# An attention stage woven into a mixture of experts on one core: value products moved to later steps, sums of the first block taken earlier, transposes cut into 64-row halves

## The chip, the cores and the metric

The kernel runs on one core of a Trainium2 chip. The metric is the device time of one execution in microseconds (us), lower is better. Several runs of one kernel are taken and their median is quoted.

## The reference, cut to what matters

Three layers follow each other: a gated linear attention, a mixture of four experts, and a gated two-layer network.

```
for t in range(S):                       # attention: B=4, H=8 heads, S=768, D=48
    state = alpha[:, :, t, :, None] * state + einsum('bhd,bhe->bhde', k[:, :, t], v[:, :, t])
    y[:, :, t] = einsum('bhd,bhde->bhe', q[:, :, t], state)
x = y.transpose(0, 2, 1, 3).reshape(3072, 384)
p = domain_probs / (domain_probs.sum(-1) + 1e-9)
out = sum over e of p[:, e] * (relu(x @ w1[e]) @ w2[e])    # 4 experts, 384 -> 1024 -> 384
h = out @ w_in                                             # 384 -> 2048
return (h * clip(h + 3, 0, 6) / 6) @ w_out                 # 2048 -> 384
```

All of it is float32. The kernel splits each float32 operand of the two networks into a high and a low part, and makes three TensorE products of the parts.

## The kernel before

**The two networks** work on 6 blocks of 512 tokens. A step takes 128 hidden columns: `mm1` (L800) makes nine products into the tile `ph`, ScalarE writes the high part `hh` (L808), VectorE the low part `hl` (L811), and `mm2` (L859), one step later, makes nine products of `hh` and `hl` into the sums `po`. In `mm2` the third product of each column group is the first that reads `hl`. Steps on one expert are a visit; at its end `finish` multiplies the sums by the routing weight on VectorE (L902: t<-po,pb), which also frees the `po` banks for the next visit. In phase 0 every block takes 14 steps, a visit of 8 and one of 6. Block 0 is run as two halves of 256 tokens, 14 short steps each, since its tokens come from attention only little by little. The `ph` of block 0 has two banks, later ones have one, so that there `mm1` waits for `hl` of the step before.

**The attention** is cut into 12 units of 256 positions (3 for each batch). The class `Attention` writes its work as named pieces, in three tables of seven entries each (L48 to L56). Entry k of `GROUP` and `BETWEEN` is issued at the end of a step, and entry k of `CHUNK` in the step behind it, after that step's `mm1` and its `hl`. So a unit takes seven steps, which are called k0 to k6 here. A sign says whose piece it is: `-` the unit before, `+` the unit after. What the pieces do:

- k0 and k1: `T_tp`, `T_k`, `T_q` transpose alphas, keys and queries on TensorE into PSUM (ptt, pkt, pqt); ScalarE copies them to SBUF in a scattered order (L313, L328). `L2 L3` and `ST` (L458, L479) finish the output `py` of the unit before. `X` is a pair of one-column ScalarE copies (`met`, L471) for which `ST` waits. `tls` is on VectorE.
- k1 to k4: `Sc` copies `kc`, `qc` on ScalarE (L346), `Su` scales `kt`, `qt` in place on VectorE (L356, two instructions), `C` makes the score products (L368), one level of a tree per step. `Su0` waits for the copies of `T_q`, since `kc` stands behind them on ScalarE.
- `M0`, `M2` mask the scores (L380), `K` transposes keys back (pk, L392), `U` makes state updates into `pu` (L404), which reuses the bank that M2 reads, `Z` chains four states on VectorE (L427, L433), `Y` transposes `y8` by pairs of 64-row products (py, L442).
- In `CHUNK`: `y0` to `y5` are the products with the values (L253 to L280), which need `Y` of k6 only; `p`, `r`, `u`, `kk`, `kq`, `tp` prepare the next unit (L190 to L247).

In all engines but GpSimd the instructions stand in the order of the program, so a piece delays whatever is issued behind it on its engine. Attention has four PSUM banks. Two hold `py` from k6 until the copy in `A` in the step of k2. At k0 the other two are the banks of `pu`, which `Z` reads last. Units 1 to 4 lie in block 0, units 5 to 11 in blocks 1 to 4; unit 0 is a prologue.

The loop over steps decides where the pieces go:

```
low = mm1(vi, f)
low()
if rest:
    at.rest(rest.pop(0))
...
if done:
    mm2(*done)
```

Of the kernel before, what the change touches and what calls it, by code (L numbers as in the profile page):

```python
# [18 lines left out]
P = 128  # L19


class Attention:
# [20 lines left out]
    U = 256  # L43
    W = (4, 8, 16, 32)
    T = 64
# [3 lines left out]
        "T_tp T_k0 -L2 -L3 T_k1", "-ST T_q0 T_q1", "C0", "C1", "C2", "C3 K0 K1", "U Y L0 L1",  # L49
# [5 lines left out]
        "y0 y1 y2 y3 y4 y5", "-A +p0 +r0", "+p1 +p2 +r1", "-R +u0", "+u1 +cp +kk +kq", "+tp +p3 +r2", "-XS",  # L55
# [235 lines left out]
    def tree(self, n):  # L291
# [7 lines left out]
        s = {"tls": [], "kc": {}, "qc": {}, "pas": {}, "asb": {}, "ktok": {}, "sb": []}  # L299
# [16 lines left out]
        def T(src, tag, half):  # L316
            if half == 0:
                s[tag] = wk(tag, [P, 2, NP, P])
            pt = self.ps(f"p{tag}{half}_{n}")
            for i in range(4):  # L320
                pe.transpose(pt[:, P * i : P * i + P], src[:, 4 * half + i].rearrange("p h d -> p (h d)"), self.ident)  # L321
            out = s[tag].rearrange("p j r (c i) -> p j i c r", i=8)[:, :, 4 * half : 4 * half + 4]
            src_ = pt.rearrange("p (i j c r) -> p j i c r", i=4, j=2, r=NP)
            for j in range(2):
                if n == 0 and tag == "qt":
                    nc.vector.tensor_copy(out[:, j], src_[:, j])
                else:
                    nc.scalar.copy(out[:, j], src_[:, j])  # L328
# [213 lines left out]
def tile_gla__then__moe__then__moe2(  # L542
# [497 lines left out]
    for vi, vv in enumerate(visits):  # L1040
# [16 lines left out]
        for f in range(len(vv["steps"])):  # L1057
# [85 lines left out]
```

## Time and profile before

| what | value |
|---|---|
| median of 3 runs | 1397.3 us (1396.82 to 1398.92) |
| profiled execution, own time | 1398.23 us |
| its span, first to last instruction | 1396.3 us |
| TensorE busy in the span | 1363.5 us (98%) |
| VectorE busy | 843.9 us (60%) |
| ScalarE busy | 453.2 us (32%) |
| mean granted TensorE clock | 0.99 of full speed |

The profile is of one execution. Busy shares are means over stages with quite different limits: attention ends at about 480 us of the span, block 0 at about 182 us. A wait in the rows stands in square brackets before an instruction, with what released it.

### The profile page before, as it was taken

Reading aid. Unit: us, or ns where it says so; the run is one execution under the profiler, and the core shown is the slowest. Engines: PE = TensorE matmul, PEld = TensorE weight load, DVE = VectorE, ACT = ScalarE, POOL = GpSimd, SP = SyncE. Lnnn points to the kernel's source line nnn. Section 1 sums busy time; section 2 is a strip of 40 time slices with the busy share of each in tenths; the row PEclk is TensorE's granted clock in tenths of the full one; section 3 lists DMA queues with packets and bytes.
Section 4 is the critical chain, followed back from the end, with each engine's and each line's share of the span. In section 5 each row is a group of like instructions: output and inputs, shape, how many; then the busy total and the mean of one; then the engine's idle time right before and its main releaser. Section 6 shows DMA issues by size and latency. Waiting matters only on the chain.

```text
span 1396.3 us, 25745 instructions
## 1 busy us (share of the span) xinstructions
PE 1363.5 (98%) x10674; PEld 1143.5 (82%) x10674; DVE 843.9 (60%) x1526; ACT 453.2 (32%) x821; POOL 83.3 (6%) x125
## 2 busy tenths in 40 slices
PE   7699999999999999999999999999999999999998
PEld 6688888888878888888888888888888888888898
DVE  8899977768776258757666666635543333334332
ACT  3555444443344133211111111113333333333333
POOL 2000000000000001121111111100000000000000
PEclk9889999999999999999999999999999999999999
DMA  6654554345442247524242332313302020202010
GB/s 195 175 146 134 156 140 121 99 119 144 134 120 80 75 148 233 162 64 140 64 130 86 96 109 84 117 64 121 102 0 46 1 46 0 46 1 46 1 23 23
DMA packets 156548, 132.31 MB, mean 95 GB/s; under 512 B 65040, under 2 KB 138256, under 8 KB 156432
## 3 DMA queue, kind: packets, MB, share of 16 engines
q1 hardware_dynamic: 156432, 130.68, 32.6%
q8 instruction: 83, 1.36, 0.4%
q14 instruction: 33, 0.27, 0.1%
HBM read 100.71 MB, written 34.65 MB: 97 GB/s over the span
## 4 chain that ended last, share of the span: by engine, by line
PE 89%; DVE 7%; issue 1%; DMA 1%; ACT 1%; SPq 0%; DVEq 0%
PE ph L800 41%; PE po L859 38%; PE po L861 2%; PE py L458 2%; PE py L479 1%; PE pa L368 1%; PE pu L404 1%; PE pkt L321 1%; DVE qt L356 1%; DVE kt L356 1%; PE pk L392 1%; DVE hl L811 1%; DVE asb L380 1%; PE pqt L321 1%; DVE dg L247 1%
## 5 line engine op out<-in xcount | busy, mean ns | idle before, releaser
L859 PE MATMUL po<-hl,w1h 128*128 128x512 f32 (+1 forms) x858 | 326.4, 380 | 6.5 <-DVE hl L811 6.5
L859 PE MATMUL po<-hh,w1h 128*128 128x512 f32 (+1 forms) x858 | 326.4, 380 | 4.6 <-DVE t L902 4.5
L859 PE MATMUL po<-hh,w1l 128*128 128x512 f32 (+1 forms) x858 | 326.0, 380 | 0.0
L808 ACT ACTIVATE hh<-ph 128x512 fp32r<-128x512 f32 (+1 forms) x206 | 117.5, 570 | 523.1 <-PE ph L800 515.9
L811 DVE SCALAR_TENSOR_TENSOR hl<-ph,hh 128x512 fp32r<-128x512 f32 (+1 forms) x206 | 134.5, 653 | 245.4 <-ACT hh L808 245.4
L800 PE MATMUL ph<-xh,w0h 128*128 128x512 f32 (+1 forms) x906 | 255.9, 391 | 2.7 <-ACT xh L775 2.4
L800 PE MATMUL ph<-xh,w0l 128*128 128x512 f32 (+1 forms) x906 | 247.6, 382 | 0.0
L800 PE MATMUL ph<-xl,w0h 128*128 128x512 f32 (+1 forms) x906 | 247.2, 381 | 0.2 <-DVE xl L776 0.2
L800 PEld LDWEIGHTS ph<-xh,w0l 128*128 128x128 f32 x906 | 167.8, 190 | 33.1
L800 PEld LDWEIGHTS ph<-xl,w0h 128*128 128x128 f32 x906 | 167.6, 190 | 33.2 <-DVE xl L776 0.5
L859 PEld LDWEIGHTS po<-hl,w1h 128*128 128x128 f32 x858 | 162.5, 189 | 38.0 <-DVE hl L811 7.4
L859 PEld LDWEIGHTS po<-hh,w1h 128*128 128x128 f32 x858 | 162.5, 189 | 35.6 <-ACT hh L808 2.9
L800 PEld LDWEIGHTS ph<-xh,w0h 128*128 128x128 f32 x906 | 163.4, 190 | 33.8 <-ACT xh L775 2.6
L859 PEld LDWEIGHTS po<-hh,w1l 128*128 128x128 f32 x858 | 162.6, 189 | 30.3
L823 DVE SCALAR_TENSOR_TENSOR g<-g,ph 128x512 f32<-128x512 f32 (+1 forms) x97 | 66.2, 684 | 170.9 <-ACT g L819 170.9
L819 ACT ACTIVATE g<-ph,three 128x512 f32<-128x512 f32 (+1 forms) x97 | 66.2, 684 | 184.8 <-PE ph L800 184.8
L826 DVE SCALAR_TENSOR_TENSOR hl<-g,hh 128x512 fp32r<-128x512 f32 (+1 forms) x97 | 66.5, 687 | 66.7 <-ACT hh L824 66.7
L824 ACT ACTIVATE hh<-g 128x512 fp32r<-128x512 f32 (+1 forms) x97 | 61.0, 630 | 74.6 <-DVE g L823 74.6
L669 POOL TENSOR_TENSOR sq<-hc 128x256 f32<-128x256 f32 x48 | 34.5, 718 | 634.7 <-DVE hc L668 632.7
L902 DVE TENSOR_TENSOR t<-po,pb 128x512 f32<-128x512 f32 (+1 forms) x82 | 52.6, 656 | 0.0
L346 ACT COPY kc<-kt 128x512 f32<-128x512 f32 x48 | 30.3, 631 | 63.2 <-PE pa L368 46.8
L684 POOL TENSOR_TENSOR a<-a,hc 128x256 f32<-128x256 f32 x48 | 38.8, 808 | 184.6 <-DVE hc L683 184.6
(106 smaller groups left out, 1210.5 us busy)
## 6 DMA issues: line engine op xcount, KB each, us to landing
rx<-x_d SPq DMA_DIRECT2D x36, 384.0 KB
vl<-vd SPq DMA_DIRECT2D x96, 96.0 KB
rw<-in_moe_w_dram SPq DMA_DIRECT2D x21, 384.0 KB
pb<-p_d SPq DMA_DIRECT2D x28, 256.0 KB
raw<-in_moe_w_in_dram SPq DMA_DIRECT2D x24, 256.0 KB
raw<-in_moe_w_out_dram SPq DMA_DIRECT2D x24, 256.0 KB
acc_d<-t SPq DMA_DIRECT2D x20, 256.0 KB
rq<-in_q_dram SPq DMA_DIRECT2D x24, 192.0 KB
```

What stands on the lines that cost most here:

```text
L346: nc.scalar.copy(c.rearrange("p x (b w) -> p (x b) w", w=self.W[l]), halves(z, l, x))
L669: nc.gpsimd.tensor_tensor(sq, hc, hc, op=mul)
L684: nc.gpsimd.tensor_tensor(a, a, hc, op=add)
L800: pe.matmul(ph[:, 0:n], w[:, j, fs], x[:, j, cs], start=(o == 0 and j == 0), stop=(o == 2 and j == KT - 1),)
L808: nc.scalar.activation(hh[:, 0:n], ph[:, 0:n], AF.Relu)
L811: nc.vector.scalar_tensor_tensor(hl[:, 0:n], ph[:, 0:n], 0.0, hh[:, 0:n].bitcast(F32), op0=ALU.max, op1=sub)
L819: nc.scalar.activation(g[:, c], ph[:, c], AF.Relu, bias=three)
L823: nc.vector.scalar_tensor_tensor(g[:, c], g[:, c], 6.0, ph[:, c], op0=ALU.min, op1=mul)
L824: nc.scalar.activation(hh[:, c], g[:, c], AF.Copy, scale=1.0 / 6.0)
L826: nc.vector.scalar_tensor_tensor(hl[:, c], g[:, c], 1.0 / 6.0, hh[:, c].bitcast(F32), op0=mul, op1=sub)
L859: pe.matmul(accs[vi][m][:, 0:n], w[:, z, ms], h[:, 0:n], **fl)
L902: nc.vector.tensor_tensor(t[:, 0:n], po[:, 0:n], pb, op=mul)
```

## The change

Three edits. In `CHUNK`, `y2` to `y5` leave entry 0 for entries 1 to 4, `kq` goes from entry 4 to 5, and the load of the next unit's values moves from entry 1 to entry 4, behind the last piece that reads them. In the loop, where a visit of block 0 ended with the step before, `mm2` with its sums is now issued ahead of the attention's `CHUNK` piece. `T` and `K` no longer make eight 128-row transposes in two halves, each with its own bank; they make 16 products of 64 rows, the upper 64 partitions into one bank and the lower into the other, in turn, and the copies follow after all 16. `T_k` now comes behind `L2 L3` as one piece.

```diff
@@ -46,13 +46,13 @@
     H = 7
 
     GROUP = (
-        "T_tp T_k0 -L2 -L3 T_k1", "-ST T_q0 T_q1", "C0", "C1", "C2", "C3 K0 K1", "U Y L0 L1",
+        "T_tp -L2 -L3 T_k", "-ST T_q", "C0", "C1", "C2", "C3 K", "U Y L0 L1",
     )
     BETWEEN = (
         "-X tls", "Sc0 Su0", "Sc1 Su1", "Sc2 M0 Su2", "Sc3 Su3", "M2", "Z0 Z1 Z2 Z3",
     )
     CHUNK = (
-        "y0 y1 y2 y3 y4 y5", "-A +p0 +r0", "+p1 +p2 +r1", "-R +u0", "+u1 +cp +kk +kq", "+tp +p3 +r2", "-XS",
+        "y0 y1", "-A +p0 +r0 y2", "+p1 +p2 +r1 y3", "-R +u0 y4", "+u1 +cp +kk y5", "+kq +tp +p3 +r2", "-XS",
     )
 
     def __init__(self, ctx, tc, q, k, v, alpha, y_d, psum_pool, psum_tag, reload, split):
...
@@ -313,19 +313,25 @@
                 nc.scalar.copy(out[:, j], src[:, j])
             s["tls"].append(tl)
 
-        def T(src, tag, half):
-            if half == 0:
-                s[tag] = wk(tag, [P, 2, NP, P])
-            pt = self.ps(f"p{tag}{half}_{n}")
-            for i in range(4):
-                pe.transpose(pt[:, P * i : P * i + P], src[:, 4 * half + i].rearrange("p h d -> p (h d)"), self.ident)
-            out = s[tag].rearrange("p j r (c i) -> p j i c r", i=8)[:, :, 4 * half : 4 * half + 4]
-            src_ = pt.rearrange("p (i j c r) -> p j i c r", i=4, j=2, r=NP)
+        def T(src, tag):
+            out = s[tag] = wk(tag, [P, 2, NP, P])
+            pts = [self.ps(f"p{tag}{j}_{n}") for j in range(2)]
+            for i in range(8):
+                for j in range(2):
+                    js = slice(64 * j, 64 * j + 64)
+                    pe.matmul(
+                        pts[j][:, 64 * i : 64 * i + 64],
+                        src[js, i].rearrange("p h d -> p (h d)"),
+                        self.ident[js, js],
+                        start=True, stop=True, is_transpose=True,
+                    )
             for j in range(2):
+                to = out[:, j].rearrange("p r (c i) -> p i c r", i=8)
+                from_ = pts[j].rearrange("p (i c r) -> p i c r", i=8, r=NP)
                 if n == 0 and tag == "qt":
-                    nc.vector.tensor_copy(out[:, j], src_[:, j])
+                    nc.vector.tensor_copy(to, from_)
                 else:
-                    nc.scalar.copy(out[:, j], src_[:, j])
+                    nc.scalar.copy(to, from_)
 
         def tls():
 
...
@@ -385,14 +391,23 @@
                 )
             s["asb"][l] = a_
 
-        def K(j):
-
-            pt = self.ps(f"pk{j}_{n}")
-            for r in range(NP):
-                pe.transpose(pt[:, P * r : P * r + P], s["kt"][:, j, r, :], self.ident)
-            kk = wk(f"ktok{j}", [P, NP, 2, 64])
-            nc.scalar.copy(kk.rearrange("p r h d -> p (r h d)"), pt)
-            s["ktok"][j] = kk
+        def K():
+
+            pts = [self.ps(f"pk{h}_{n}") for h in range(2)]
+            for x in range(2 * NP):
+                for h in range(2):
+                    hs = slice(64 * h, 64 * h + 64)
+                    pe.matmul(
+                        pts[h][:, 64 * x : 64 * x + 64],
+                        s["kt"][hs, x // NP, x % NP, :],
+                        self.ident[hs, hs],
+                        start=True, stop=True, is_transpose=True,
+                    )
+            kk = s["ktok"] = wk("ktok", [P, 2, NP, 2, 64])
+            for h in range(2):
+                nc.scalar.copy(
+                    kk.rearrange("p j r h d -> p (j r) h d")[:, :, h, :], pts[h].rearrange("p (x d) -> p x d", d=64)
+                )
 
         def Ust():
 
...
@@ -403,7 +418,7 @@
                         for c in range(2):
                             pe.matmul(
                                 pus[c][64 * h : 64 * h + 64, j, r, :],
-                                s["ktok"][j][64 * c : 64 * c + 64, r, h, :],
+                                s["ktok"][64 * c : 64 * c + 64, j, r, h, :],
                                 self.vt[64 * c : 64 * c + 64, j, 2 * r + h, :],
                                 start=True,
                                 stop=True,
...
@@ -498,9 +513,8 @@
         d = dict(
             T_tp=T_tp, tls=tls, U=Ust, Y=Y, X=X, ST=ST, A=A,
             R=lambda: self.reload(n), XS=lambda: self.split(n),
-            T_k0=lambda: T(self.kp, "kt", 0), T_k1=lambda: T(self.kp, "kt", 1),
-            T_q0=lambda: T(self.qp, "qt", 0), T_q1=lambda: T(self.qp, "qt", 1),
-            M0=lambda: M(0), M2=lambda: M(2), K0=lambda: K(0), K1=lambda: K(1),
+            T_k=lambda: T(self.kp, "kt"), T_q=lambda: T(self.qp, "qt"),
+            M0=lambda: M(0), M2=lambda: M(2), K=K,
         )
         for l in range(4):
             d[f"Sc{l}"] = lambda l=l: Sc(l)
...
@@ -531,8 +545,9 @@
         self.run(n, self.CHUNK[k])
 
         if k == 1:
+            self.load_vt(n)
+        if k == 4:
             self.load(n + 1, "v")
-            self.load_vt(n)
         if k == 5:
             self.load(n + 2, "qka")
             self.load_vd(n + 1)
...
@@ -954,8 +969,8 @@
             pe.matmul(idle[:, 0:P], at.ident, at.ident, start=True, stop=True)
 
     busy(30)
-    u("p0 p1 p2 u0 u1 cp kk kq tp T_tp T_k0 T_k1")
-    u("T_q0 tls T_q1")
+    u("p0 p1 p2 u0 u1 cp kk kq tp T_tp T_k")
+    u("T_q tls")
     busy(6)
     u("p3 r0")
     at.load(1, "qka")
...
@@ -1061,14 +1076,17 @@
             serve()
             low = mm1(vi, f)
             low()
-            if rest:
+            pend.append((vi, f))
+            done = pend.pop(0) if len(pend) > 1 else None
+            sums = done and visits[done[0]]["n"] < NB and done[1] == len(visits[done[0]]["steps"]) - 1
+            if rest and not sums:
                 at.rest(rest.pop(0))
             if late:
                 next(dec, None)
-            pend.append((vi, f))
-            done = pend.pop(0) if len(pend) > 1 else None
             if done:
                 mm2(*done)
+            if rest and sums:
+                at.rest(rest.pop(0))
             at_step += 1
             if period < len(ends):
                 while g < begun + (ends[period] - begun) * at_step // (2 * S0):
```

VectorE, unit 4, step k1 in block 0 with the start of k2 (hl_7 and hl_0 are the low parts of two steps, y and pr belong to y0 to y5, kt and qt to Su0, w and dg to p0 and r0). Before:

```order
L811 SCALAR_TENSOR_TENSOR hl_7_2407<-ph_7_2396,hh_7_2406 128x256
L253 TENSOR_TENSOR y_112<-rv_1950,dg_4_1948 128x2x8x48
L257 TENSOR_TENSOR pr_4_2411<-rv_1950,dg_4_2017 128x384
L259 TENSOR_TENSOR y_112<-y_112,pr_4_2411 128x2x4x48
L267 TENSOR_TENSOR pr_4_2414<-rv_1950,dg_4_2190 128x4x96 x2
L274 TENSOR_TENSOR pr_4_2414<-pr_4_2414 128x8x48
L280 TENSOR_TENSOR y_112<-y_112,pr_4_2414 128x2x2x48 x2
L356 TENSOR_TENSOR kt_2339<-kt_2339,tl_4_2333 128x128x4
L356 TENSOR_TENSOR qt_2453<-qt_2453,tl_4_2333 128x128x4
L811 SCALAR_TENSOR_TENSOR hl_0_2485<-ph_0_2474,hh_0_2484 128x256
L190 TENSOR_TENSOR w_5_2496<-rq_2192,rk_2195 128x768
L247 TENSOR_REDUCE dg_5_2498<-w_5_2496 128x16
```

With the change:

```order
L253 TENSOR_TENSOR y_112<-rv_2194,dg_4_2011 128x2x8x48
L257 TENSOR_TENSOR pr_4_2493<-rv_2194,dg_4_2079 128x384
L259 TENSOR_TENSOR y_112<-y_112,pr_4_2493 128x2x4x48
L362 TENSOR_TENSOR kt_2447<-kt_2447,tl_4_2409 128x128x4
L362 TENSOR_TENSOR qt_2529<-qt_2529,tl_4_2409 128x128x4
L826 SCALAR_TENSOR_TENSOR hl_0_2567<-ph_0_2556,hh_0_2566 128x256
L917 TENSOR_TENSOR t_0_2576<-po_0_2024,pb_1665 128x256
L917 TENSOR_TENSOR t_1_2578<-po_0_2024,pb_1665 128x256
L917 TENSOR_TENSOR pb_1665<-po_1_2025,pb_1665 128x256
L190 TENSOR_TENSOR w_5_2592<-rq_2268,rk_2271 128x768
L247 TENSOR_REDUCE dg_5_2594<-w_5_2592 128x16
L267 TENSOR_TENSOR pr_4_2596<-rv_2194,dg_4_2266 128x4x96
```

Su0 now follows y1; the three sums, which stood behind dg, stand ahead of p0; the first of the four moved value pieces stands behind dg, ahead of Su1.

TensorE, T_q of unit 4 between ST and mm1 of the next step. Before:

```order
L479 MATMUL py_3_2247<-qt_1903,sc_148 64x64 x8
L321 MATMUL pqt_4_2454<-ident,qp 128x128 x4
L321 MATMUL pqt_4_2461<-ident,qp 128x128 x4
L800 MATMUL ph_0_2474<-xh_0_719,w0h_1161 128x256 x3
L800 MATMUL ph_0_2474<-xh_0_719,w0l_1162 128x256 x3
```

With the change, the last five of its 16 products:

```order
L322 MATMUL pqt_4_2531<-ident,qp 128x64
L322 MATMUL pqt_4_2530<-ident,qp 128x64
L322 MATMUL pqt_4_2531<-ident,qp 128x64
L322 MATMUL pqt_4_2530<-ident,qp 128x64
L322 MATMUL pqt_4_2531<-ident,qp 128x64
L815 MATMUL ph_0_2556<-xh_0_744,w0h_1199 128x256 x3
L815 MATMUL ph_0_2556<-xh_0_744,w0l_1200 128x256 x3
```

Both banks are complete only with the last two products.

ScalarE, copies around k0 and k1 of unit 4 (tl, kt, qt are the copies of T_tp, T_k, T_q). Before:

```order
L313 COPY tl_4_2333<-ptt_2334 128x2x16x4 x2
L328 COPY kt_2339<-pkt_4_2340 128x4x16x4 x2
L328 COPY kt_2339<-pkt_4_2379 128x4x16x4 x2
L471 COPY met<-py_3_2246 128x1
L471 COPY met<-py_3_2247 128x1
L808 ACTIVATE hh_7_2406<-ph_7_2396 128x256
L328 COPY qt_2453<-pqt_4_2454 128x4x16x4 x2
L328 COPY qt_2453<-pqt_4_2461 128x4x16x4 x2
L346 COPY kc_4_2468<-kt_2339 128x512
```

With the change:

```order
L313 COPY tl_4_2409<-ptt_2410 128x2x16x4 x2
L334 COPY kt_2447<-pkt_4_2448 128x8x16x4
L334 COPY kt_2447<-pkt_4_2449 128x8x16x4
L486 COPY met<-py_3_2322 128x1
L486 COPY met<-py_3_2323 128x1
L823 ACTIVATE hh_7_2488<-ph_7_2478 128x256
L334 COPY qt_2529<-pqt_4_2530 128x8x16x4
L334 COPY qt_2529<-pqt_4_2531 128x8x16x4
L352 COPY kc_4_2550<-kt_2447 128x512
```

Four copies of 256 elements a partition became two of 512, in the same places.

## Rows read from the trace of the kernel before

**Rows 1.** Stretches: length, busy us of PE, PEld, DVE, ACT, POOL, PEclk, DMA share, GB/s

```profile
60.00:95.00 35.00, 30.36 (x511) 27.93 (x511) 31.84 (x63) 17.77 (x39) 0.00 (x0) 0.85 0.55 152
95.00:128.00 33.00, 29.50 (x543) 27.42 (x543) 30.19 (x62) 16.80 (x39) 0.00 (x0) 0.90 0.50 137
128.00:180.00 52.00, 48.07 (x936) 44.40 (x932) 48.11 (x101) 25.00 (x60) 0.00 (x0) 0.97 0.58 159
...
210.00:480.00 270.00, 269.70 (x3623) 219.54 (x3622) 186.03 (x350) 106.31 (x221) 0.00 (x0) 1.00 0.38 108
```

**Rows 2.** Timeline of VectorE, block 0: start, us, instruction, idle before it

```profile
59.58 0.96 DVE L190 TENSOR_TENSOR w<-rq,rk 128x768 f32<-128x768 f32 x1 [1.41 <-DMA rk<-in_k_dram]
...
90.21 1.03 DVE L267 TENSOR_TENSOR pr<-rv,dg 128x384 f32<-128x384 f32 x2
91.27 0.56 DVE L274 TENSOR_TENSOR pr<-pr 128x384 f32<-128x384 f32 x1
91.87 0.63 DVE L280 TENSOR_TENSOR y<-y,pr 128x192 f32<-128x192 f32 x2
92.41 0.69 DVE L356 TENSOR_TENSOR kt<-kt,tl 128x512 f32<-128x512 f32 x1
...
126.88 0.69 DVE L356 TENSOR_TENSOR kt<-kt,tl 128x512 f32<-128x512 f32 x1 [1.87 <-ACT kc L346]
...
136.25 0.42 DVE L811 SCALAR_TENSOR_TENSOR hl<-ph,hh 128x256 fp32r<-128x256 f32 x1
...
146.08 0.35 DVE L433 TENSOR_TENSOR sc<-sd,pu 128x192 f32<-128x192 f32 x1
```

**Rows 3.** Timeline of TensorE, block 0, instructions that waited

```profile
97.60 0.55 PE L859 MATMUL po<-hh,w1h 128*128 128x256 f32 x1 [2.71 <-DVE t L902]
...
136.73 0.39 PE L859 MATMUL po<-hl,w1h 128*128 128x256 f32 x1 [1.18 <-DVE hl L811]
...
160.88 0.36 PE L859 MATMUL po<-hh,w1h 128*128 128x256 f32 x1 [1.81 <-DVE t L902]
```

**Rows 4.** Chain that ended last, block 0 and block 1: start, us, what

```profile
149.67 1.07 PE ph L800 x9
...
207.74 2.08 PE ph L800 x9
...
212.95 0.64 PE py L442 x16
213.59 1.09 PE py L458 x64
214.68 2.26 PE ph L800 x9
...
218.99 0.22 PE ptt L309 x2
219.20 0.44 PE pkt L321 x4
...
220.73 0.59 PE pkt L321 x4
...
227.45 1.02 PE pqt L321 x8
```

**Rows 5.** ScalarE copies by line and shape: busy us, mean ns, idle before

```profile
L328 ACT COPY kt<-pkt 128x256 f32<-128x256 f32 x48 | 27.2, 690 | 5.3 <-PE pkt L321 5.3
...
L313 ACT COPY tl<-ptt 128x128 f32<-128x128 f32 x24 | 7.4, 414 | 8.5 <-PE ptt L309 8.3
L471 ACT COPY met<-py 128x1 f32<-128x1 f32 x24 | 2.8, 212 | 6.5 <-PE py L458 6.5
```

**Rows 6.** Timeline of ScalarE, copies of T_q, unit 3

```profile
124.29 2.13 ACT L328 COPY qt<-pqt 128x256 f32<-128x256 f32 x4 [3.23 <-PE pqt L321]
```

**Rows 7.** Timeline of TensorE and VectorE, first visit end of block 1

```profile
237.51 0.68 DVE L811 SCALAR_TENSOR_TENSOR hl<-ph,hh 128x512 fp32r<-128x512 f32 x1
...
238.25 0.97 PE L800 MATMUL ph<-xh,w0h 128*128 128x512 f32 x3
```

More of the change, by code (lines that the diff above doesn't have):

```diff
@@ L298, in tree @@
         NL = len(self.W)
-        s = {"tls": [], "kc": {}, "qc": {}, "pas": {}, "asb": {}, "ktok": {}, "sb": []}
+        s = {"tls": [], "kc": {}, "qc": {}, "pas": {}, "asb": {}, "sb": []}
         def wk(tag, shape):
@@ L971, in tile_gla__then__moe__then__moe2 @@
     busy(5)
-    u("C3 y2 M2 K0 K1 y3 y4 y5 U Y L0 L1 L2 L3 X Z0 Z1 Z2 Z3 ST")
+    u("C3 y2 M2 K y3 y4 y5 U Y L0 L1 L2 L3 X Z0 Z1 Z2 Z3 ST")
     sw(0, 0)
@@ L988, in tile_gla__then__moe__then__moe2 @@
     at.load(2, "qka")
-    u("T_tp T_k0 T_k1 tls", 1)
+    u("T_tp T_k tls", 1)
     u("XS")
```

## The prediction

> **What bounds the kernel now.** I read the stretches first, then the timelines of VectorE and TensorE in block 0, then the chain that ended last. In the stretches the reader is to see two regimes. From 210 to 480 us TensorE is busy 269.7 of 270 us: whatever leaves TensorE there leaves the time, if no wait comes in its place. In block 0 (60 to 180 us) no engine is full, but VectorE is nearest: 110.1 us busy of 120 [rows 1]. There the two engines hand work to and fro, and the timelines tell who is late.
>
> VectorE is late from Su0 to the end of the Zs. In unit 3 it starts Su0 at 126.88 and the low part of k4 at 136.25 [rows 2]; TensorE stands 1.18 us for that low part [rows 3]. I call this moment H. VectorE is early from the Zs to the next Su0: it stood 1.87 us before Su0 of unit 3, waiting for the copy `kc` [rows 2]. Between those two points the path runs over TensorE and ScalarE: T_k, two half-products, ST, T_q, the copies of T_q, `kc`. This gap is where y0 to y5 stand now. So the value products lie where VectorE would otherwise wait.
>
> **The change part by part.** VectorE's durations are distances between starts, since neighbours overlap a little. y2 and y3 take 91.27 - 90.21 = 1.06 us (0.53 each), y4 0.60, y5 92.41 - 91.87 = 0.54; together 2.20 [rows 2].
>
> *Value products, Su0 to H.* y2 (k2) and y3 (k3) come ahead of the low part of k4. VectorE has no spare time on this stretch, so H comes 1.06 us later in each of units 1 to 4. Unit 1 might seem to gain, its y2 to y5 being gone from the front. But its next piece, p0, waits for the key load until 59.58, having stood 1.41 us [rows 2]; VectorE only stands longer, and the y2 and y3 come behind that wait. 4 x 1.06 = **+4.2 us**. Bounds: 0, if each low part had this much slack, and 2.2 per unit, all that is moved.
>
> *Value products, H to Z.* y4 and y5 add 1.14 us; kq leaves k5 and joins k6, still ahead of the Zs, so it counts nothing here. Z2, which frees the bank for ptt, ended at 146.08 + 0.35, 10.18 us behind H [rows 2]. It now ends at H + 11.32. Then ptt 0.22, L2 L3 1.09 (64 small products, as in the row of py L458) and T_k 0.64 follow [rows 4]: H + 13.3. Before, T_k ended and mm1 began at 149.67 - 136.25 = H + 13.4 [rows 2, 4]. So the shorter T_k just pays for this delay: **-0.1**, four times -0.4.
>
> *Transposes on TensorE.* The 64-row products were not there for keys and queries, but Y makes the same: 16 in 0.64 us; eight 128-row ones take 1.02 (T_q) or 0.44 + 0.59 (T_k) [rows 4]. Against that, mm1 takes 2.26 behind 64-row products and 2.08 behind 128-row ones [rows 4], 0.18 more. Net -0.20 for each T_q and K; for T_k it is 0.22 + 0.44 + 1.09 + 0.59 + 2.08 against 0.22 + 1.09 + 0.64 + 2.26, -0.21. Bounds of the 16 products: 0.27 us (at the pace of the 64 products of L458, 1.09 / 64 each) and 1.02 (no faster than now). I take 0.64, the same shape. By the Trainium skill, TensorEngine Tiling (Array Packing), section Theoretical Speedup, a dimension of 64 gives up to 2x, which would make them 0.51; Y's row shows less. By that figure every transposition would save 0.13 us more.
>
> *Copies.* A scattered copy takes 414 ns for 128 elements and 690 for 256, so 276 more per 128: some 1.24 us for 512 [rows 5]. Four of 256 take 2.13 back to back, 0.48 apart [rows 6]; two of 512, about 1.03 apart, take 2.27. They also begin about 0.2 later, because the first copy waited for four transposes and now waits for all 16 products. So `kc` and Su0 come 0.35 us later behind T_q (bounds 0 and 0.8, a copy of twice 690). The same rows bear on a rule of the Trainium skill that speaks against this edit: TensorEngine Tiling (Array Packing), section PSUM Bottleneck, says that tiling speeds TensorE but not the evacuation, which may become the bottleneck. The trace agrees: 2.13 us of copies stand behind 1.02 of transposes, and Su0 waits for the copies. In my sum T_q's gain is therefore worth nothing in block 0.
>
> *Behind T_k* both copies now run after it: 0.1 + 2.27 + 0.25 for the two one-column copies (212 ns each, overlapping) [rows 5] = 2.6 us until ST may start, while two half-products take 1.26 + 1.08 = 2.34. (1.26 is the 1.07 of row 149.67 [rows 4] with 0.19 for what stands ahead of it; mm2 has nine such products as well.) A new wait of 0.3 in block 0, none later, where a full step's products take twice as long.
>
> *One gap in block 0* thus gains 0.19 (mm1) + 0.3 + 0.35 = 0.8 us, for the gaps into Su0 of units 2, 3, 4: +2.5. Block 0: 4.2 - 0.4 + 2.5 + 0.2 (mm1 behind the last T_k) = **+6.5 us**.
>
> *Sums ahead.* At two visit ends of block 0 TensorE stood 2.71 and 1.81 us for the sums [rows 3]. p0 (0.96 us, [rows 2]) and r0, which I estimate to be as long, less the overlap of neighbours, 1.85 us in all, leave their front. But all this still has to be done by VectorE before H, so TensorE arrives earlier and waits there: I take **0**. Bounds: 0, and 1.85 + 1.81 = 3.7 us. The clock was below full there (0.85, 0.90, 0.97 in the three stretches, [rows 1]); shorter waits might raise it, which I leave to a rival.
>
> *Blocks 1 to 4.* T_q and K of unit 5 and all three of units 6 to 11 are 20 transpositions: 20 x -0.20 = **-4.0 us**. VectorE is busy 186 of 270 us there [rows 1], so it has room in most steps. It has none in the step behind a visit end (units 6, 8, 10, in k2), where three sums of 512 columns stand: the low part started at 237.51 and took 0.68, to 238.19, and mm1, which needs its bank, started at 238.25 [rows 7]. There y2 (0.53) and the 0.35 of the copies come ahead of it, and y3 (0.53) ahead of the next, which had no slack either; and the 0.2 that T_q saves isn't seen. 3 x 1.6 = **+4.8**. Together +0.8.
>
> *Loads.* Two loads of values a unit move three steps back in SP's order, ahead of the next queries and keys; the loads `vt` and `vl` behind them come earlier. Values are first read by y0, over two steps later: 0. If this cover failed, a wait like the 1.41 us for keys [rows 2] would come with each unit. kq later: T_q reads it two steps on, 0. Prologue: the copies of queries there wait for all products, which are shorter by as much: 0.
>
> **Sum.** 6.5 + 0.8 = +7.3 on the profiled execution's 1398.23 us: 1405.5. The median of the runs lies 0.9 below that execution, so I say **1405 us**.
>
> **The rivals.**
> (a) *TensorE is what is late in block 0, and the sums decide.* Then its two waits shrink (-3.7), eleven transpositions of block 0 save 0.2 each (-2.2), and with blocks 1 to 4 (-4.0) it gives 1397.3 - 9.9 = 1387 us. For it: the two longest waits at the sums, and the low clock in these stretches. Against it: VectorE's 110 of 120 us and the 1.18 us at H. It decides from the point where the wait at H is gone although 1.06 us were put ahead of it. Chance 0.15.
> (b) *The delays are half absorbed.* Only units 3 and 4 show their 1.06, the gaps grow by half, and visit ends find slack: 2.1 + 1.2 - 4.0 = -0.7, about 1397. For it: VectorE could use idle moments that I counted as needed. Against it: from 126.88 to 136.25 [rows 2] its instructions follow each other without a stand. Chance 0.17.
> (c) *The clock.* The wait at H grows from 1.18 to 2.2 us. Behind the wait of 2.71 and the other of 1.81 lies part of the stretches with a mean clock of 0.90 and 0.97 [rows 1, 3]; if the longer waits drop the clock from 2.4 to 1.2 GHz in units 3 and 4 as well, nine products and what follows up to `pu` take up to 2 us longer each: 1405 + 4 = 1409. Chance 0.16.
> (d) *Products of 64 rows at twice the pace.* 20 x 0.13 = 2.6 less: 1402. Against it Y's row. Chance 0.05. It is the result that the page named above would give.
>
> **How the numbers follow.** The forecast has 0.47. About 0.2% (2.8 us) is what a measurement of this kernel can tell from no change. Faster: (a), and a share of (b), 0.20. Same (1394.5 to 1400.1): most of (b) and the forecast's low edge, 0.15. Slower: 0.65. The likeliest case alone, by the bounds of the copies and of y2 and y3, spans 1400 to 1409. The range goes to 1394 below, which takes in (b), and to 1411 above, which takes in (c); (a) is left out with the tails.
>
> **What would show it.** In the profile after: VectorE idle before Su0 of units 2 to 4 longer by some 2 us each; TensorE's wait for the low part at H at 2 us or more; Su0 to H longer by 1.06; the sums' waits under 1 us; 16 products in about 0.64 and mm1 at 2.26 behind them; two copies in 2.3; block 0 ending 6 to 7 us later; TensorE waiting 0.5 to 1 us behind three visit ends. Block 0 ending no later than before would make the prediction wrong.

## The result, and the profile after

| | before | after |
|---|---|---|
| median of 6 runs | 1397.45 us (1396.82 to 1398.92) | 1405.42 us (1404.95 to 1406.41) |
| profiled execution: its own time, span, mean granted clock | 1398.23, 1396.3 us, 0.990 | 1405.06, 1403.0 us, 0.985 |

The ratio of after to before is 1.0057, with a 95% interval of 1.0044 to 1.007: slower by 0.57%, about 8 us by the medians, against 7.3 forecast. The two profiled executions, from which all rows come, are 6.83 us apart.

The stretches of the changed kernel, cut as in [rows 1]:

```profile
60.00:95.00 35.00, 28.76 (x535) 26.41 (x535) 30.46 (x61) 17.23 (x34) 0.00 (x0) 0.90 0.55 157
95.00:128.00 33.00, 29.02 (x537) 26.61 (x535) 29.09 (x61) 15.22 (x32) 0.00 (x0) 0.90 0.52 138
128.00:180.00 52.00, 45.55 (x777) 41.62 (x776) 44.80 (x93) 24.02 (x53) 0.00 (x0) 0.88 0.50 141
210.00:480.00 270.00, 266.87 (x3789) 214.32 (x3789) 186.71 (x358) 107.74 (x201) 0.00 (x0) 1.00 0.39 110
```

In the third stretch TensorE is 2.5 and VectorE 3.3 us less busy, and the clock is 0.88 where it was 0.97. From 210 us on TensorE is 3.1 us short of full. VectorE in block 0, by its timeline; the rows answer to [rows 2]:

```profile
58.74 0.96 DVE L190 TENSOR_TENSOR w<-rq,rk 128x768 f32<-128x768 f32 x1 [0.62 <-DMA rk<-in_k_dram]
...
92.71 0.69 DVE L362 TENSOR_TENSOR kt<-kt,tl 128x512 f32<-128x512 f32 x1 [1.53 <-ACT kc L352]
...
106.84 0.42 DVE L826 SCALAR_TENSOR_TENSOR hl<-ph,hh 128x256 fp32r<-128x256 f32 x1
...
128.45 0.69 DVE L362 TENSOR_TENSOR kt<-kt,tl 128x512 f32<-128x512 f32 x1 [3.52 <-ACT kc L352]
...
131.84 0.55 DVE L267 TENSOR_TENSOR pr<-rv,dg 128x384 f32<-128x384 f32 x1
132.31 0.68 DVE L362 TENSOR_TENSOR kt<-kt,tl 128x512 f32<-128x512 f32 x1
...
138.76 0.42 DVE L826 SCALAR_TENSOR_TENSOR hl<-ph,hh 128x256 fp32r<-128x256 f32 x1
...
161.09 0.69 DVE L362 TENSOR_TENSOR kt<-kt,tl 128x512 f32<-128x512 f32 x1 [2.30 <-ACT kc L352]
...
172.59 0.42 DVE L826 SCALAR_TENSOR_TENSOR hl<-ph,hh 128x256 fp32r<-128x256 f32 x1
...
196.34 0.69 DVE L362 TENSOR_TENSOR kt<-kt,tl 128x512 f32<-128x512 f32 x1 [3.73 <-ACT kc L352]
```

and of the kernel before, Su0 of units 4 and 5:

```profile
156.59 0.69 DVE L356 TENSOR_TENSOR kt<-kt,tl 128x512 f32<-128x512 f32 x1 [0.67 <-ACT kc L346]
...
189.40 0.69 DVE L356 TENSOR_TENSOR kt<-kt,tl 128x512 f32<-128x512 f32 x1 [2.67 <-ACT kc L346]
```

The first row is p0 of unit 1. The rows with `kt` that waited are Su0 of units 2, 3, 4 and 5, those at 131.84 and 132.31 are y2 and the Su1 behind it in unit 3, and the rows with `hl` are H. VectorE now stands 1.53, 3.52 and 2.30 us ahead of Su0 of units 2 to 4, where it stood 0, 1.87 and 0.67 before: 1.5 to 1.7 more (I had said some 2). Ahead of Su0 of unit 2 it hadn't stood at all, so there y0 to y5 did not lie wholly in waiting time. A value piece shifts its successor by 132.31 - 131.84 = 0.47 us, so y2 and y3 cost 0.94, not 1.06. TensorE in block 0 and at the first visit end of block 1, instructions that waited, against [rows 3, 7]:

```profile
96.04 0.36 PE L874 MATMUL po<-hh,w1h 128*128 128x256 f32 x1 [0.85 <-DVE t L917]
...
139.23 0.38 PE L874 MATMUL po<-hl,w1h 128*128 128x256 f32 x1 [2.02 <-DVE hl L826]
...
173.06 0.39 PE L874 MATMUL po<-hl,w1h 128*128 128x256 f32 x1 [2.01 <-DVE hl L826]
...
242.07 0.47 PE L874 MATMUL po<-hh,w1h 128*128 128x512 f32 x1 [0.38 <-DVE t L917]
245.17 0.96 PE L815 MATMUL ph<-xh,w0h 128*128 128x512 f32 x3 [0.16 <-DVE hl L826]
250.68 0.96 PE L815 MATMUL ph<-xh,w0h 128*128 128x512 f32 x3 [0.51 <-DVE hl L826]
```

The waits for sums shrank from 2.71 to 0.85 us and, in unit 4, from 1.81 to nothing that counts. The waits at H of units 3 and 4 are at 2 us; that of unit 2 is 1.42. The last three rows make 1.05 us, at the upper end of the 0.5 to 1 that I had named; they come again at the two other visit ends.

One table of VectorE's starts splits block 0; it is read from such rows of each kernel:

| us | Su0 to H, units 2, 3, 4 | H to next Su0, units 1, 2, 3, 4 |
|---|---|---|
| before | 13.20, 9.37, 10.56 | 23.25, 21.27, 20.34, 22.25 |
| after | 14.13, 10.31, 11.50 | 23.45, 21.61, 22.33, 23.75 |

In unit 1 H came 0.10 us later. Su0 of unit 5, where the table ends, moved from 189.40 to 196.34: 6.9 us. Behind it little is left. The T_k of units 5 and 11 were 246.73 us apart and are 246.92 now. So block 0 holds the loss of the profiled execution.

### The profile page after: what moved, and what is told of

It reads as the page before. It is cut to its first block, busy times and chain, and to the rows that moved or that the text cites. A ratio compares the mean times of both kernels' runs of the same rounds, so it can differ in the third digit from the quotient of the medians.

```text
span 1403.0 us, 26262 instructions
## 1 busy us (share of the span) xinstructions
PE 1362.8 (97%) x10962; PEld 1138.9 (81%) x10962; DVE 841.2 (60%) x1524; ACT 452.9 (32%) x775; POOL 82.8 (6%) x125
## 4 chain that ended last, share of the span: by engine, by line
PE 88%; DVE 8%; ACT 2%; issue 1%; DMA 1%; SPq 0%; DVEq 0%
PE ph L815 40%; PE po L874 37%; PE po L876 2%; PE py L473 2%; PE py L494 1%; PE pa L374 1%; ACT qt L334 1%; DVE qt L362 1%; PE pu L419 1%; DVE asb L386 1%; DVE kt L362 1%; DVE dg L247 1%; DVE hl L826 1%; PE pkt L322 1%; DVE rq L193 1%
## 5 line engine op out<-in xcount | busy, mean ns | idle before, releaser
L362 DVE TENSOR_TENSOR kt<-kt,tl 128x512 f32<-128x512 f32 x48 | 32.9, 686 | 38.2 <-ACT kc L352 38.2
```

The costliest lines, as they stand in the source:

```text
L362: tt(zv, zv, tlv[:, :, 1 - x].unsqueeze(2).to_broadcast([P, nb, w]), op=mul)
```

## The experiments

They were timed in three sets, each beside the kernel before, whose median was 1397.86 to 1397.95 us. My theory after the result: the value pieces between Su0 and H are paid in full, the transposes gain, the sums ahead move a wait, and something behind H in units 3 and 4 costs more than I had counted.

### The change without its value pieces

```diff
-        "y0 y1", "-A +p0 +r0 y2", "+p1 +p2 +r1 y3", "-R +u0 y4", "+u1 +cp +kk y5", "+kq +tp +p3 +r2", "-XS",
+        "y0 y1 y2 y3 y4 y5", "-A +p0 +r0", "+p1 +p2 +r1", "-R +u0", "+u1 +cp +kk +kq", "+tp +p3 +r2", "-XS",
...
         if k == 1:
+            self.load(n + 1, "v")
             self.load_vt(n)
-        if k == 4:
-            self.load(n + 1, "v")
```

> The change without its first edit: y0 to y5 stand together in entry 0 again, kq in entry 4, the value loads in entry 1; transposes and sums as changed. Theory A (the value pieces leave a gap in which VectorE waits anyway, and the rest of the change is a gain of a few us, nearly all in blocks 1 to 4): 20 transpositions x -0.2 = -4.0, visit ends behind block 0 give back 3 x 0.35, block 0 within 1 us: 1394 us, 3 below the kernel before. Rival B (the transposes with their later, longer copies are what costs): 1401 us or more. Rival C (the sums ahead are worth the two waits and the clock behind them): 1390 us or less.

Measured: 1395.26 us (1394.05 to 1396.69), ratio 0.9982 [0.9973, 0.9991]. The two other parts together make the kernel slightly faster; all of the loss comes with the value pieces and their load.

### The value pieces alone

On the kernel before:

```diff
-        "y0 y1 y2 y3 y4 y5", "-A +p0 +r0", "+p1 +p2 +r1", "-R +u0", "+u1 +cp +kk +kq", "+tp +p3 +r2", "-XS",
+        "y0 y1", "-A +p0 +r0 y2", "+p1 +p2 +r1 y3", "-R +u0 y4", "+u1 +cp +kk y5", "+kq +tp +p3 +r2", "-XS",
...
         if k == 1:
-            self.load(n + 1, "v")
             self.load_vt(n)
+        if k == 4:
+            self.load(n + 1, "v")
```

> The kernel before with the first edit alone: y2 to y5 and kq and the value loads moved, transposes and sums as before. Theory A: block 0 gains 4 x 0.94 from y2 and y3 ahead of the low part of k4, less 0.8 for the key load of unit 2, plus 2 to 3 for y4, y5 and the lower clock behind the longer waits; three visit ends cost 1.06 each: 1397.5 + 8 = 1405 us. Rival B: within 2 us of the kernel before. Rival C: within 2 us as well, since the sums are not touched.

Measured: 1410.54 us (1408.87 to 1411.84), ratio 1.0088 [1.0075, 1.0102]: 12.7 us by the medians, where the whole change costs 8. Block 0 ended 8.6 us later (mm1 behind T_k of unit 5). No theory came near: A had 1405. The steps of my sum seem to give the 8.6 for the pieces alone: without the shorter T_k, y4 and y5 delay each unit in full, 4 x (1.06 + 1.14) = 8.8. That is in part luck. In units 2 to 4 Su0 to H grew by 0.94 and H to the next Su0 by 1.0 to 1.2 us; but in unit 1 H came 0.32 us later and the next Su0 a further 2.35, with a mean granted clock of 0.79 from 84 to 92 us.

### The sums ahead alone

```diff
+            pend.append((vi, f))
+            done = pend.pop(0) if len(pend) > 1 else None
+            sums = done and visits[done[0]]["n"] < NB and done[1] == len(visits[done[0]]["steps"]) - 1
-            if rest:
+            if rest and not sums:
                 at.rest(rest.pop(0))
...
             if done:
                 mm2(*done)
+            if rest and sums:
+                at.rest(rest.pop(0))
```

> The kernel before with the sums of block 0 taken ahead, nothing else. Theory A (VectorE has to do p0 and r0 before the low part of k4 all the same): TensorE's waits for the sums of 2.71 and 1.81 us fall under 1 us, and come back at the next low parts; 1396 to 1398 us. Rival C (the waits for the sums decide, with the clock behind them): 1392 us or less.

Measured: 1399.57 us (1398.78 to 1402.31), ratio 1.0017 [1.0008, 1.0026]: a little slower. TensorE's waits in unit 2, in the place of the single 2.71 us of before:

```profile
95.45 0.36 PE L859 MATMUL po<-hh,w1h 128*128 128x256 f32 x1 [0.85 <-DVE t L902]
...
100.15 0.39 PE L859 MATMUL po<-hl,w1h 128*128 128x256 f32 x1 [1.25 <-DVE hl L811]
105.79 0.39 PE L859 MATMUL po<-hl,w1h 128*128 128x256 f32 x1 [2.42 <-DVE hl L811]
```

The wait became three, and the longest now stands at H. The clock moved with it. Windows from 96 to 104 and 104 to 112 us (the columns are those of [rows 1]), of the kernel before:

```profile
96.00:104.00 8.00, 6.40 (x58) 6.09 (x59) 7.83 (x14) 3.17 (x6) 0.00 (x0) 0.57 0.67 190
104.00:112.00 8.00, 7.69 (x134) 7.03 (x136) 7.96 (x17) 4.53 (x11) 0.00 (x0) 1.00 0.45 141
```

and of the sums alone:

```profile
96.00:104.00 8.00, 6.13 (x100) 5.32 (x98) 7.90 (x13) 2.79 (x6) 0.00 (x0) 1.00 0.66 187
104.00:112.00 8.00, 6.21 (x65) 5.85 (x65) 7.96 (x17) 4.65 (x11) 0.00 (x0) 0.79 0.41 137
```

Before, TensorE was slow ahead of H, where VectorE is what is late. Now it is slow behind H, where TensorE's own products lead to T_k. H to the next Su0 grew from 21.27 to 22.85 us. How much of that is the clock wasn't measured: an idle stretch of 0.86 us at 115.74 us, for which the profile names no releaser, lies there too.

### The transposes alone

The functions `T` and `K` of the change with the names that call them, on the kernel before:

```diff
-        "T_tp T_k0 -L2 -L3 T_k1", "-ST T_q0 T_q1", "C0", "C1", "C2", "C3 K0 K1", "U Y L0 L1",
+        "T_tp -L2 -L3 T_k", "-ST T_q", "C0", "C1", "C2", "C3 K", "U Y L0 L1",
...
+                        start=True, stop=True, is_transpose=True,
...
```

> The kernel before with the 64-row transposes alone. Theory A: -4.0 for the 20 transpositions in blocks 1 to 4, +1.0 for the later copies at three visit ends, block 0 within 1 us: 1394.5 us. Rival B (the transposes cost): 1401 us or more.

Measured: 1393.98 us (1393.62 to 1395.98), ratio 0.9972 [0.9962, 0.9982]: faster than both kernels. Su0 of units 3 and 4, by VectorE's timeline:

```profile
126.57 0.69 DVE L362 TENSOR_TENSOR kt<-kt,tl 128x512 f32<-128x512 f32 x1 [1.51 <-ACT kc L352]
...
155.56 0.69 DVE L362 TENSOR_TENSOR kt<-kt,tl 128x512 f32<-128x512 f32 x1
```

H to the next Su0 takes 23.14, 20.93, 19.62 and 21.60 us: shorter by up to 0.7, where I had the gap longer. In unit 4 VectorE no longer stands ahead of Su0. Between the T_k of units 5 and 11 this kernel takes 2.59 us less.

### TensorE kept busy at H

In the changed kernel, ahead of the product that waits at H, in units 3 and 4 (`po_[1][:, 1]` is half a bank that nobody reads; `spare` keeps the banks of a visit from its first step on):

```diff
+        po_ = spare.get(vi)
...
             for o, (w, h) in enumerate(((wh, hh), (wl, hh), (wh, hl))):
+                if half and m == 0 and o == 2 and period == 1 and at_step in (4, 11):
+                    for _ in range(14):
+                        pe.matmul(po_[1][:, 1], wh[:, z, ms], hh[:, 0:n], start=False, stop=False, skip_group_check=True)
```

> The changed kernel, with 14 products of 256 columns into half a bank that nobody reads, at the moment H of units 3 and 4, where TensorE waited 2.02 and 2.01 us for the low part; at 0.12 us each they take 1.7 us of those waits. Theory A (the clock): what units 3 and 4 lost between H and T_k (15.1 us where units 1 and 2 kept their 15.7 and 13.9) is the half clock behind those two waits; then the granted clock stays at 1.0 from 136 to 148 us and from 172 to 184 us, H to T_k falls by 1.2 to 1.7 us in each, and the time from 1405.4 to about 1402.5 us. Theory B (VectorE's own pieces): the loss is y4, y5 and kq ahead of the Zs; nothing changes, 1405.4 us. Theory C: the products come too late for the low part and delay what follows: 1406 us or more.

Measured: 1403.05 us (1402.65 to 1404.45), ratio to before 1.0037 [1.0023, 1.005]. Windows from H of units 3 and 4 on, of the changed kernel:

```profile
136.00:148.00 12.00, 9.98 (x152) 9.13 (x152) 11.39 (x26) 3.91 (x10) 0.00 (x0) 0.72 0.47 139
172.00:184.00 12.00, 10.94 (x222) 10.06 (x223) 11.37 (x28) 3.91 (x10) 0.00 (x0) 0.72 0.55 167
```

and of this one, with TensorE's row at H and Su0 of unit 4:

```profile
136.00:148.00 12.00, 11.12 (x269) 10.22 (x259) 11.90 (x28) 3.82 (x10) 0.00 (x0) 1.00 0.48 138
172.00:184.00 12.00, 10.84 (x258) 9.79 (x261) 11.55 (x29) 4.02 (x11) 0.00 (x0) 1.00 0.56 164
```
```profile
137.71 1.84 PE L875 MATMUL po<-hh,w1h 128*128 128x256 f32 x14
139.88 0.39 PE L880 MATMUL po<-hl,w1h 128*128 128x256 f32 x1 [0.33 <-DVE hl L827]
```
```profile
160.03 0.69 DVE L362 TENSOR_TENSOR kt<-kt,tl 128x512 f32<-128x512 f32 x1 [2.29 <-ACT kc L352]
```

The low part came no sooner (Su0 to H is 10.32 us), so only the waiting was filled. The clock stayed at 1.00, and H to the next Su0 fell from 22.33 to 20.62 us in unit 3 and from 23.75 to 22.55 in unit 4: 2.9 us. That is the price of the clock, shown by itself. The times of the two kernels differ by 2.4 us, since the clock also fell elsewhere. Behind the Zs of unit 1, of the changed kernel:

```profile
80.00:88.00 8.00, 6.17 (x130) 5.54 (x131) 5.17 (x16) 3.96 (x9) 0.00 (x0) 1.00 0.85 218
```

and of this one:

```profile
80.00:88.00 8.00, 6.15 (x103) 5.44 (x102) 4.49 (x13) 3.21 (x7) 0.00 (x0) 0.79 0.89 231
```

There H to the next Su0 took 24.85 us instead of 23.45, while ptt still started 13.6 us behind H: all of the 1.4 us was lost between the Zs and Su0, where T_k and T_q are on the path. With H of unit 1 0.8 us sooner, 2.9 - 1.4 + 0.8 = 2.3 us.

### y2 and y3 back

In the changed kernel, with y4, y5 and kq still behind H:

```diff
-        "y0 y1", "-A +p0 +r0 y2", "+p1 +p2 +r1 y3", "-R +u0 y4", "+u1 +cp +kk y5", "+kq +tp +p3 +r2", "-XS",
+        "y0 y1 y2 y3", "-A +p0 +r0", "+p1 +p2 +r1", "-R +u0 y4", "+u1 +cp +kk y5", "+kq +tp +p3 +r2", "-XS",
```

> The changed kernel with y2 and y3 back in the entry of y0 and y1; y4, y5 and kq stay spread, behind H. Theory A (what stands between Su0 and H is paid in full, and the clock with it): Su0 to H shorter by 0.94 us in units 2 to 4 (-2.8), the waits at H back at 1.2 us and the clock at 1.0 behind them (-2.6), the step behind three visit ends without y2 and without y3 behind it (-2.6): about 1397.4 us. Theory B (no part of it is the clock): 1400 us. Theory C (it matters only how many pieces leave the gap, not where they go): half of the 10 us that spreading cost stays, 1400.5 us, with the waits at H still above 1.5 us.

Measured: 1396.85 us (1394.29 to 1398.38), ratio to before 0.9987 [0.9978, 0.9996]: 8.6 us less than the change. TensorE at H of unit 3, and the window behind it:

```profile
136.26 0.39 PE L874 MATMUL po<-hl,w1h 128*128 128x256 f32 x1 [1.18 <-DVE hl L826]
```
```profile
136.00:148.00 12.00, 11.05 (x273) 10.00 (x277) 11.65 (x30) 4.44 (x12) 0.00 (x0) 1.00 0.52 164
```

That is theory A. Su0 to H is 9.38 and 10.57 us again in units 3 and 4, and H to the next Su0 20.60 and 22.56, though y2 and y3 stand in that gap: there VectorE does them while it would wait. In unit 3 the wait at H is 1.18 and the clock 1.00. In unit 4 the wait is 1.55 and the clock over 168 to 176 us 0.79, yet the 22.56 us are those of the kernel with TensorE kept busy (22.55): this drop cost nothing. Between the T_k of units 5 and 11 lie 244.15 us, as in the transposes alone. So two pieces of 0.47 us, on the wrong side of H, make nearly all of the loss. The other pieces, with the later load, cost some 1.6 us by the medians (1396.85 against 1395.26).

### The transposes with the later value load

On the transposes alone:

```diff
         if k == 1:
-            self.load(n + 1, "v")
             self.load_vt(n)
+        if k == 4:
+            self.load(n + 1, "v")
```

> The transposes alone with the load of values three entries later, as the change has it. Theory A (the keys of unit 1 share the queues with the value load): p0 of unit 1 starts about 0.8 us sooner than the 59.76 us of the transposes alone, its wait for keys is below 0.3 us, and the time falls from 1394.0 to about 1393.2 us. Theory B (the keys land when they land): p0 as before and 1394.0 us. Theory C (the later values are missed): a new wait of y0 for the values, 1395 us or more.

Measured: 1393.87 us (1392.69 to 1395.12), ratio 0.9968 [0.9956, 0.9979], as the transposes alone. p0 of unit 1 started at 60.19 us, behind a wait of 0.79 for its keys, not sooner than the 59.76 of the transposes alone. The order of the loads costs and gains nothing that shows. That p0 started 0.84 us sooner in the profiled execution of the change than before isn't explained by it; over all the kernels it started between 57.99 and 60.19.

### Part of VectorE's work on GpSimd

On the transposes alone; r1 stands one entry later:

```diff
-            tt(q, q, a, op=mul)
+            (nc.gpsimd if 1 <= n <= 4 else nc.vector).tensor_tensor(q, q, a, op=mul)
...
-            tt(wtile(1)[:, 0 : 8 * D].rearrange("p (x d) -> p x d", d=D), q2[:, :, 1, :], k2[:, :, 0, :], op=mul)
+            (nc.gpsimd if 1 <= n <= 4 else nc.vector).tensor_tensor(wtile(1)[:, 0 : 8 * D].rearrange("p (x d) -> p x d", d=D), q2[:, :, 1, :], k2[:, :, 0, :], op=mul)
...
-        "y0 y1 y2 y3 y4 y5", "-A +p0 +r0", "+p1 +p2 +r1", "-R +u0", "+u1 +cp +kk +kq", "+tp +p3 +r2", "-XS",
+        "y0 y1 y2 y3 y4 y5", "-A +p0 +r0", "+p1 +p2", "-R +u0 +r1", "+u1 +cp +kk +kq", "+tp +p3 +r2", "-XS",
```

> The transposes alone, with p1 and p2 of units 1 to 4 on the idle GpSimd and r1 one entry later, so that 2.06 us of VectorE's work leave the stretch from Su0 to H. Theory A (that stretch sets block 0): Su0 to H shorter by 1.5 to 2 us in units 2 and 4, by the 1.2 us of the wait at H in unit 3, where TensorE then decides; the two waits for sums of 3.36 and 1.80 us shrink; about 1390 us. Theory B (TensorE decides block 0): the waits only move, 1393.5 to 1394.5 us. Theory C (GpSimd and VectorE get in each other's way): VectorE's pieces beside p1 and p2 get longer, and the time is 1394 us or more.

Measured: 1393.26 us (1392.93 to 1394.3), ratio 0.9964 [0.9952, 0.9977], little better, if at all, than the transposes alone (1393.98). GpSimd and VectorE in unit 3:

```profile
128.67 1.83 POOL L193 TENSOR_TENSOR rq<-rq,ra 128x768 f32<-128x768 f32 x1 [29.32 <-DVE w L190]
130.57 1.35 POOL L197 TENSOR_TENSOR w<-rq,rk 128x384 f32<-128x384 f32 x1
```
```profile
129.44 1.61 DVE L362 TENSOR_TENSOR kt<-kt,tl 128x512 f32<-128x512 f32 x1
130.97 1.51 DVE L362 TENSOR_TENSOR qt<-qt,tl 128x512 f32<-128x512 f32 x1
```

Beside GpSimd's two multiplications VectorE's took 1.61 and 1.51 us instead of 0.69 and 0.68. Of the 2.06 us taken off, these two rows give back 1.75; Su0 to H is 9.09 us instead of 9.37. In unit 3 that is theory C's mechanism, though the time lies below its 1394. In unit 2 only one such multiplication got longer (1.42 us), and Su0 to H fell from 13.16 to 11.92. In unit 4 no piece runs on GpSimd, since the p1 and p2 there are those of unit 5; r1 alone left, and Su0 to H fell from 10.57 to 9.98. What was gained was lost behind H: H to the next Su0 grew by 0.23, 0.86 and 0.73 us in units 2 to 4. r1, which shifts its successor by 0.46 us, stands there now; the rest of that loss is open.

### The change without the sums ahead

In the changed kernel:

```diff
-            if rest and not sums:
+            if rest:
                 at.rest(rest.pop(0))
...
-            if rest and sums:
-                at.rest(rest.pop(0))
```

> The changed kernel without the part on the sums (the spread value pieces and the transposes stay). Theory A (the sums ahead only move TensorE's wait from the sums to the low parts, and what they cost alone, some 1.5 us, they cost here too): the waits for sums in units 2 and 4 are back at 2 to 3 us, those for low parts of the same units fall, and the time is 1403.5 to 1405.5 us. Theory B (with the pieces spread VectorE is so late that sums ahead pay): 1407 us or more, the sum of what the parts gave alone (12.7 less 3.5 on 1397.9).

Measured: 1404.5 us (1401.49 to 1405.21), ratio 1.0039 [1.0026, 1.0052]. The sums ahead gain nothing here either; whether they cost 1 us is within the intervals. As theory A has it, TensorE's waits for the sums of units 2 and 4 are back at 3.16 and 2.27 us, and its waits at H there are 0.29 us and none. Its profiled execution, the fastest of its five, happened to be a control for the clock. TensorE at H of unit 3, and the window:

```profile
138.60 0.39 PE L874 MATMUL po<-hl,w1h 128*128 128x256 f32 x1 [2.02 <-DVE hl L826]
```
```profile
136.00:148.00 12.00, 9.89 (x235) 8.97 (x235) 11.90 (x27) 3.92 (x11) 0.00 (x0) 1.00 0.49 150
```

The same wait of 2.02 us, and no drop. H to the next Su0 took 20.60 us in unit 3 and 22.55 in unit 4, as with TensorE kept busy.

### The change without the transposes

In the changed kernel, with `T` and `K` of before:

```diff
-        "T_tp -L2 -L3 T_k", "-ST T_q", "C0", "C1", "C2", "C3 K", "U Y L0 L1",
+        "T_tp T_k0 -L2 -L3 T_k1", "-ST T_q0 T_q1", "C0", "C1", "C2", "C3 K0 K1", "U Y L0 L1",
...
```

> The changed kernel with the transposes of before (spread pieces and sums ahead stay). Theory A (products of 64 rows save the same 0.17 us each wherever TensorE is the bound, and shorten the way from the Zs to the next Su0 in block 0, with or without the spread): 1405.4 + 3.5 to 5 = 1409 to 1410.5 us, blocks 1 to 4 longer by 2.6 us between the T_k of units 5 and 11. Theory B (the spread hides what the transposes save, VectorE being late): 1407 us or less.

Measured: 1409.02 us (1407.97 to 1411.68), ratio 1.0084 [1.007, 1.0098]: the transposes are worth 3.6 us within the change. Between the T_k of units 5 and 11 it takes 249.51 us, against 246.92: 2.59, as with the transposes alone.

### The transposes, TensorE kept busy at H of unit 1

On the transposes alone:

```diff
+                if half and m == 0 and o == 2 and period == 0 and at_step == 4:
+                    for _ in range(16):
+                        pe.matmul(po_[1][:, 1], wh[:, z, ms], hh[:, 0:n], start=False, stop=False, skip_group_check=True)
```

> The transposes alone, with 16 products of 256 columns into the unread half bank at the moment H of unit 1, where TensorE waited 2.42 us and the granted clock behind it was 0.73 and 0.84 in two stretches of 4 us. Theory A (a long wait at H costs the clock of the stretch to T_k, in whichever unit): the clock stays at 1.0 from 68 to 76 us, H to T_k of unit 1 falls by 0.8 to 1.3 us, and the time from 1394.0 to about 1393 us. Theory B (unit 1 waits there for its loads and for VectorE, the clock is beside the point): 1394.0 us, the gain being lost in a longer wait behind it.

Measured: 1393.76 us (1393.3 to 1395.93), ratio 0.9972 [0.9961, 0.9984]. No gain, theory B: the clock from 68 to 76 us rose from 0.79 to 1.00, but H to mm1 behind T_k is 14.70 us in both. The time stands again a little later, where TensorE waits for the Zs:

```profile
81.48 0.41 PE L309 MATMUL ptt<-ident,tp 128*128 128x128 f32 x2 [1.49 <-DVE sc L448]
```

In unit 1 VectorE is late behind H as well, so a full clock only lengthens this wait.

## Why the prediction was right, and where its terms were not

The direction, the place and the mechanism held: VectorE is late from Su0 to H, early behind the Zs, and pieces that cross H cost. The total was right within 1 us, but partly by luck: terms that were too large made up for the clock, for which I had no term.

- **Su0 to H, 4 x 1.06 = 4.2.** Shown for units 2 to 4 (y2 and y3 back takes it away), mis-sized: 0.94 each, since I had taken 0.53 a piece from the distance between a pair's start and the piece behind it, and a piece alone shifts its neighbours by 0.47. In unit 1 it failed: H moved by 0.10, as p0's wait for keys was 0.84 us over sooner; why the keys came sooner is open. Sum 2.9.
- **H to Z and T_k, -0.1 each.** Held within 0.1 in unit 3 with the full clock: T_k ended at H + 13.42 before, and at H + 13.48 with TensorE kept busy. Behind H of unit 3 y4, y5 and kq then cost 20.62 - 19.62 = 1.0 us (TensorE kept busy, against the transposes alone), where I had 1.14; and the transposes alone take 20.34 - 19.62 = 0.7 off, where my steps, the gap with them, make 0.4. Both together lengthen H to the next Su0 by 0.20, 0.34, 0.28 and 0.30 us in units 1 to 4 (the last two with TensorE kept busy), where I had 0.7.
- **The gap, 3 x 0.8.** Mis-sized. Its 0.19 for mm1 behind 64-row products is there: 1.27 us (the chain's row at 153.95, shown below) against 1.07 [rows 4] for nine products of 256. The 0.3 for the one-column copies and the 0.35 for T_q's copies are not. ScalarE in unit 3 to 4:

```profile
153.99 2.13 ACT L334 COPY kt<-pkt 128x512 f32<-128x512 f32 x2 [1.09 <-PE pkt L322]
155.88 0.24 ACT L486 COPY met<-py 128x1 f32<-128x1 f32 x2
...
158.52 2.11 ACT L334 COPY qt<-pqt 128x512 f32<-128x512 f32 x2 [2.11 <-PE pqt L322]
```

  The copies of T_k and of `met` end at 156.12, when the half-products end too (ST starts at 156.22). Two copies of 512 take 2.11, not 2.27: one takes 1178 ns, while I had added 2 x 276 to 690. And T_q, 0.69 in place of 1.02, gives back what the later start takes.
- **The clock, 0 in my sum, rival (c).** This is the failed step. The waits at H grew to 2.02 and 2.01 us, as forecast, and behind them TensorE was granted a mean of 0.72 over 12 us. That is partly 1.2 instead of 2.4 GHz. Keeping it busy shows the price: 1.7 us in unit 3 and 1.2 in unit 4, together 2.9, against the 4 of the rival. The change without the sums ahead, in whose profiled execution the clock stayed at 1.00 by itself, gives the same two stretches within 0.02 us. The forecast and the rival both happened, and smaller terms made room for it: block 0 of the profiled execution measures 2.9 (Su0 to H) + 1.1 (H to the next Su0) + 2.9 = 6.9 us against my 6.5.
- **The sums ahead, 0.** Nearly right: no gain inside the change, and alone a ratio of 1.0017. The waits move to the low parts, as I argued; that a wait at H can cost the clock, I hadn't counted.
- **Blocks 1 to 4, -4.0 + 4.8 = +0.8.** Both halves too large. Between the T_k of units 5 and 11 lie 18 transpositions; without the three new waits of 0.17 at visit ends, they save 2.59 + 0.5 = 3.1, or 0.17 each where I had 0.20. The pieces cost 246.92 - 244.15 = 2.8 us at three visit ends, 0.9 each: y2 and y3 at 0.47, which y2 and y3 back takes away whole, and nothing for the copies, where I had 1.6.
- **Products of 64 rows, 0.64 us for 16, with 2.26 for mm1 behind.** Right: 0.64 to 0.69, and 2.27. From the chain of the changed kernel:

```profile
153.95 1.27 PE ph L815 x9
...
226.88 0.65 PE pkt L322 x16
227.52 2.27 PE ph L815 x9
...
233.84 0.69 PE pqt L322 x16
```

  Rival (d), 0.51, is out. The factor of up to 2 that the Trainium skill gives (TensorEngine Tiling (Array Packing), Theoretical Speedup) isn't reached here: 0.64 to 0.69 against 1.02.
- **Loads, 0.** Right: beside the transposes, the later value load changes nothing.

Rival (a) is out: in the change the waits at H are still there, and with the sums ahead and the transposes alone (the change without its value pieces) TensorE waited 2.42, 2.42, 1.18 and 1.55 us at H of units 1 to 4. Rival (b) had the gaps nearly right and the rest wrong.

## What to carry to other kernels

A piece that is moved to another place of an engine's order was free here only where that engine waited; the trace shows on which side of the critical hand-over the place is, and 0.94 us on the wrong side cost 2.1 and 2.6 us in the two units where the other engine's clock fell behind the wait that they lengthened. A part of a change that gains (here the transposes, 4 us) is worth running alone. When a wait has been shifted several times and the time hasn't moved, ask which engine is late in that stretch, before and behind the hand-over.

## What was not expected of the hardware

- The same wait of 2.02 us at the same place had different sequels: the granted clock over 136 to 148 us was 0.72 in the change, 0.86 in it without the transposes and in the value pieces alone, 1.00 in it without the sums ahead. Which of them comes isn't settled by these runs.
- A drop of the clock cost only where TensorE's work is what is late: 1.7 and 1.2 us behind H of units 3 and 4 of the change, 1.4 behind the Zs of unit 1 with TensorE kept busy in units 3 and 4; but nothing right behind H of unit 1 in the transposes alone, nor behind H of unit 4 with y2 and y3 back.
- VectorE's multiplications of 512 columns took 1.4 to 1.6 us instead of 0.69 while GpSimd multiplied; in unit 3 that took back 1.75 us of the 2.06 that had been taken off it. The Trainium skill (GPSIMD Engine Reference, 1. Specifications) says that the two contend where VectorE has two inputs in SBUF; the trace agrees, and gives the size.
